# Tanh in place in bf16, the feed-forward's residual parked in DRAM, an eighth P slot with PV begun one round later, and retuned scheduler constants

## The chip, the cores and the metric

One core of a Trainium2 chip runs the whole kernel. The metric is the device time in microseconds (us) of one execution. PE is TensorE's matmul, PEld its weight load, DVE VectorE, ACT ScalarE, POOL GpSimd and SP SyncE, which issues the DMAs. Lines such as L708 are lines of the kernel's source; one helper records many operations, so the tile names beside a line say which operation it is. All the changed kernel's lines are one to seven higher than those of the kernel before: the exponential is L708 before and L709 after.

A median says how fast a kernel is, and a profile says where one execution spent its time.

## The reference

A transformer layer on 2048 tokens of 1024 features, 32 heads of 32, feed-forward width 3584, in bf16:

```python
qkv = (x @ wqkv).reshape(B, S, 3, H, Dh) ...          # on layernorm(x)
scores = jnp.einsum("bhqd,bhkd->bhqk", q, k) * scale
p = _softmax(scores, axis=-1)
o = jnp.einsum("bhqk,bhkd->bhqd", p, v)
h = x + o.reshape(B, S, D) @ wo
g = _gelu(jnp.einsum("bsd,df->bsf", _layernorm(h), w1) + b1)   # tanh form
h2 = h + jnp.einsum("bsf,fd->bsd", g, w2) + b2
```

## The kernel before

The program records every operation as a task with an assumed cost, lets a scheduler put the tasks of each engine in an order, and only then emits them. On the chip every engine runs its list in order. The scheduler's constants are therefore part of the kernel: they never appear in it as instructions, but they decide the order.

Attention is cut into 64 jobs (8 head groups by 8 chunks of 256 queries), each of 8 rounds. A round is one QK task (8 row-tiled matmuls), two exponentials of 128x1024 on ACT, and one PV task with its denominator (8 and 4 column-tiled matmuls). The exponentials write into a ring of P slots, from which PV reads:

```python
NPT = 7
PT, B_PT_ = sb(top, "PT", [P, NPT, 4, 512], BF, 2 * NPT)
...
EXP = (0.922, 0.907)                     # assumed cost of the two exps of a round
...
pe(fns, 0.217, reads=[B_KT[g][r], B_QT[self.slot]], ..., kind="qk", mode="row")
for q in range(2):
    t = act(lambda a, u=u, q=q: a.activation(PT[:, s, 2*q:2*q+2, :], psum[:, 2*u:2*u+2, :], ACT.Exp, ...), 1024, ...)
    t.occ = EXP[q]
```

The feed-forward of a chunk runs as background on PE between the QKs of the next chunks ("ffn1" is the matmul with w1, "ffn2" the one with w2). Its gelu takes one tanh on ACT for each block of 1024 columns:

```python
def gelu(R, c, fc, nf):
    (sq, b_sq), (th, b_th) = R.sq.next(), R.th.next()
    ... # sq = xh*xh ; sq = (sq + C2)*xh      (DVE)
    act(lambda a: a.activation(th, sq, ACT.Tanh, ...), n, reads=[b_sq], writes=[b_th], ...)
    dve(lambda v: v.scalar_tensor_tensor(xh, v4(th), 1.0, xh, ALU.add, ALU.mult), ...)
```

The scheduler for PE takes a ready QK first, then PV (a job's first PV only when PV_START rounds wait), then background:

```python
PV_START = 5
AHEAD = 0.3
HOLD = 3
...
if qk is not None:
    return qk
if pv is not None and not (state["mode"] == "full" and bg is not None and full_array(bg[1]) and waiting < HOLD):
    ...
    if free and pv is pvs[n] and (waiting >= PV_START or last or bg is None):
        ...
        return pv
if bg is not None:
    ...
    return t
return warm
...
gr.schedule(pick_pe)
```

At the start, 56 dummy matmuls keep PE busy while the first inputs arrive. Whatever background is left after the last QK runs alone at the end: the tail.

The softmax here doesn't subtract the row's maximum and nothing guards it: scores larger than these inputs give would overflow.

## Time and profile before

| | kernel before |
|---|---|
| median of 4 runs | 1102.28 us (1101.57 to 1104.14) |
| profiled span | 1102.0 us |
| first exponential | 15.52 us |
| ACT waits more than 1.5 us for the last time at | 64.61 us |
| from there to the end of the last exponential | 960.56 us, of which ACT is busy 957.19 |
| last exponential | ends at 1025.17 us |
| last exponential to end | 76.83 us |

The table reads as three stretches that add up to the span: 64.61 + 960.56 + 76.83 = 1102.0. Each has its own limit. In the lead the limit is how soon the first scores exist, in the long middle it is ACT, in the tail PE. A microsecond saved on an engine that isn't the limit of its stretch saves nothing. The prediction below shows the lines that this rests on.

### The profile page before, as it was taken

The page shows a single profiled execution, that of the slowest core. Times are in us where ns is not written, and L with a number is a line of the kernel's source. Part 1 is how long each engine was busy: PE and PEld are TensorE (multiplying, and loading weights), DVE is VectorE, ACT ScalarE, POOL GpSimd, SP SyncE. Part 2 cuts the span into 40 slices and gives each one's busy share as a digit, 9 for nine tenths or more (in the row PEclk, how much of TensorE's full clock was granted, in tenths as well). Part 3 has the DMA queues.
Part 4 walks back from the last instruction along what each step waited for, and adds up shares of the span by engine and source line. Part 5 has one row for each costly group of instructions (what it writes and reads, how often), then busy time and mean ns, then how long its engine had stood idle before and what let it go on. Part 6 is the DMA issues. An engine that isn't in the chain of part 4 may idle for free.

```text
span 1102.0 us, 41713 instructions
## 1 busy us (share of the span) xinstructions
PE 1059.0 (96%) x19045; PEld 588.9 (53%) x19045; DVE 823.8 (75%) x1449; ACT 1022.6 (93%) x1135; POOL 20.2 (2%) x33
## 2 busy tenths in 40 slices
PE   6999999999999989999999999999999999999999
PEld 5645565554444645454554455455545554554485
DVE  6456666666867898888788887968887888787463
ACT  5889999999999999999999999999999999999251
POOL 1100000000000000000000000000000000000000
PEclk9999999999999989999999999999999999999999
DMA  6960100012332754466837684775677487968770
GB/s 193 194 181 2 41 3 3 3 40 86 105 103 79 221 145 142 153 204 179 245 103 238 134 253 116 239 211 147 202 181 226 119 253 197 286 174 259 211 248 20
DMA packets 263161, 169.15 MB, mean 153 GB/s; under 512 B 50762, under 2 KB 260810, under 8 KB 262986
## 3 DMA queue, kind: packets, MB, share of 16 engines
q1 hardware_dynamic: 262986, 166.50, 52.8%
q8 instruction: 149, 2.44, 0.9%
q14 instruction: 26, 0.21, 0.1%
HBM read 152.31 MB, written 7.34 MB: 145 GB/s over the span
## 4 chain that ended last, share of the span: by engine, by line
ACT 78%; PE 18%; DVE 2%; DMA 1%; issue 0%; POOL 0%; DVEq 0%
ACT PT L708 74%; PE ps L504 9%; PE ps L501 5%; ACT a_th L846 4%; PE ps L700 2%; PE ps L720 2%; PE ps L739 1%; DMA w2r<-in_B_w_dram 1%; DMA hnT<-xb 1%; ACT xnT L583 0%; DMA xrb<-in_A_x_dram 0%; DVE xb L573 0%; DVE hch L785 0%; DVE stg L593 0%; DVE PS L715 0%
## 5 line engine op out<-in xcount | busy, mean ns | idle before, releaser
L708 ACT ACTIVATE PT<-ps 128x1024 bf16<-128x1024 f32 x1024 | 952.8, 1108 | 14.7 <-PE ps L700 14.2
L715 DVE TENSOR_TENSOR PS<-PT 128x1024 bf16<-128x1024 bf16 x495 | 333.1, 685 | 100.7 <-ACT PT L708 70.5
L700 PE MATMUL ps<-QT,KT 32*128 32x256 bf16 x4096 | 204.3, 274 | 14.1 <-ACT PT L708 13.1
L504 PE MATMUL ps<-hnT,w1r 128*128 128x256 bf16 x1632 | 210.8, 275 | 4.2 <-DVE gT L828 3.2
L501 PE MATMUL ps<-w2r,gT 128*32 128x512 bf16 x2832 | 192.0, 383 | 2.6 <-DVE a_os L871 1.6
L720 PE MATMUL ps<-PT,V 128*32 128x256 bf16 x4096 | 184.1, 275 | 6.6 <-ACT PT L708 5.0
L504 PEld LDWEIGHTS ps<-hnT,w1r 128*128 128x128 bf16 x1632 | 146.5, 98 | 59.3 <-issue 34.4
L700 PEld LDWEIGHTS ps<-QT,KT 32*128 32x128 bf16 x4096 | 61.3, 92 | 165.2 <-ACT PT L708 135.9
L739 PE MATMUL ps<-PS,ones 128*32 128x256 bf16 x1980 | 139.5, 276 | 1.6 <-DVE PS L715 1.6
L501 PE MATMUL ps<-xnT,Wall 128*32 128x512 bf16 x1888 | 126.7, 381 | 3.3 <-DVE stg L593 1.6
L720 PEld LDWEIGHTS ps<-PT,V 128*32 128x32 bf16 x4096 | 93.0, 96 | 66.2 <-ACT PT L708 28.9
L501 PEld LDWEIGHTS ps<-w2r,gT 128*32 128x32 bf16 x2832 | 66.1, 96 | 66.2 <-issue 26.7
L828 DVE TENSOR_TENSOR gT<-ps,b1f 128x512 bf16<-128x512 f32 x98 | 67.2, 685 | 23.0 <-PE ps L504 22.4
L504 PE MATMUL ps<-Wall,xnT 128*128 128x128 bf16 (+1 forms) x896 | 68.8, 228 | 1.2 <-ACT xnT L583 0.7
L739 PEld LDWEIGHTS ps<-PS,ones 128*32 128x32 bf16 x1980 | 52.3, 96 | 31.2 <-DVE PS L715 14.5
L501 PEld LDWEIGHTS ps<-xnT,Wall 128*32 128x32 bf16 x1888 | 43.1, 96 | 48.3 <-issue 16.0
L847 DVE SCALAR_TENSOR_TENSOR gT<-a_th,gT 128x1024 bf16<-128x1024 f32 x49 | 59.7, 1218 | 4.6 <-ACT a_th L846 4.3
L504 PEld LDWEIGHTS ps<-Wall,xnT 128*128 128x128 bf16 x896 | 55.0, 98 | 14.9 <-issue 9.5
L501 PE MATMUL ps<-w1r,OT 128*32 128x512 bf16 x896 | 60.9, 381 | 1.6 <-DVE hch L785 1.6
L844 DVE SCALAR_TENSOR_TENSOR a_sq<-a_sq,gT 128x1024 bf16<-128x1024 bf16 x49 | 59.8, 1220 | 0.6
L846 ACT ACTIVATE a_th<-a_sq 128x1024 f32<-128x1024 bf16 x49 | 56.9, 1160 | 0.0
L748 DVE STREAM_TRANSPOSE DT<-ps 128x256 f32<-128x256 f32 x64 | 28.5, 446 | 20.2 <-PE ps L739 19.8
(76 smaller groups left out, 573.4 us busy)
## 6 DMA issues: line engine op xcount, KB each, us to landing
w2r<-in_B_w_dram SPq DMA_DIRECT2D x105, 512.0 KB, 6.0
w1r<-in_B_w_dram SPq DMA_DIRECT2D x102, 512.0 KB, 4.3
w1r<-in_A_wo_dram SPq DMA_DIRECT2D x28, 512.0 KB, 4.3
wk<-in_B_w_dram SPq DMA_DIRECT2D x9, 512.0 KB, 6.2
xrb<-in_A_x_dram SPq DMA_DIRECT2D x16, 256.0 KB, 4.5
Wall<-in_A_wqkv_dram SPq DMA_DIRECT2D x16, 256.0 KB, 5.5
wv<-in_B_w_dram SPq DMA_DIRECT2D x8, 512.0 KB, 6.3
a_x<-in_A_x_dram SPq DMA_DIRECT2D x28, 128.0 KB, 4.3
```

The source lines that it names most:

```text
L501: fns.append(lambda p, j=j: p.matmul(dst(32 * j, 32 * j + 32), lhsT[:, 32 * j:32 * j + 32], rhs, start=start, stop=stop, tile_position=(0, ...
L504: t.alt = [lambda p: p.matmul(dst(0, P), lhsT, rhs, start=start, stop=stop, skip_group_check=True)]
L700: fns.append(lambda p, i=i, hh=hh, r0=r0: p.matmul(psum[:, 2 * us[hh // 2] + hh % 2, 256 * i:256 * i + 256], KT[r0:r0 + 32, g, 256 * r + P ...
L708: t = act(lambda a, u=u, q=q: a.activation(PT[:, s, 2 * q:2 * q + 2, :], psum[:, 2 * u:2 * u + 2, :], ACT.Exp, bias=0.0, scale=SCALE), 102 ...
L715: dve(lambda v: v.tensor_tensor(PS[:, z, :, :], PT[:, s, :, 0:256], PT[:, s, :, 256:512], ALU.add), c_dve(1024, 2), reads=B_PT[s], writes= ...
L720: fns.append(lambda p, i=i, hh=hh: p.matmul(psum[32 * hh:32 * hh + 32, self.bank, 0:256], V[:, g, 2 * r + i, 32 * hh:32 * hh + 32], PT[:, ...
L739: fns.append(lambda p, i=i, hh=hh, src=src: p.matmul(psum[32 * hh:32 * hh + 32, self.bank, 256:512], ones32[:, :], src[:, hh, :], start=False,
L748: dve(lambda v: v.transpose(DT[f][:], psum[:, self.bank, 256:512]), c_dve_ps(256), reads=[self.buf], writes=[B_DT[f]], prio=-1)
L828: gate[c] = dve(lambda v, xh=xh, fc=fc, grp=grp: v.tensor_tensor(xh, psum[:, grp.bank, :].rearrange("p (f n) -> p f n", f=2), b1f[:, fc:fc ...
L844: dve(lambda v: v.scalar_tensor_tensor(v4(sq), v4(sq), C2, xh, ALU.add, ALU.mult), c_dve(n), reads=[b_sq] + b_xh, writes=[b_sq], prio=1)
L846: gate[c] = act(lambda a: a.activation(th, sq, ACT.Tanh, bias=0.0, scale=K2 / 2), n, reads=[b_sq], writes=[b_th], prio=-1, kind="tanh")
L847: t = dve(lambda v: v.scalar_tensor_tensor(xh, v4(th), 1.0, xh, ALU.add, ALU.mult), c_dve(n), reads=[b_th] + b_xh, writes=b_xh, prio=1)
```

## The change

The intent is to free SBUF (tanh writes over its own input in bf16; the residual goes to DRAM and back) for an eighth P slot. With eight slots a job's PV may begin when six rounds wait, not five, so that PE can do its background in longer runs. At the same time the scheduler's constants were retuned and the warm-up was made longer.

```diff
-    NPT = 7
+    NPT = 8
...
-    hch, B_hch_ = sb(ffn, "hch", [P, 2, 2, D], BF, 8)
-    B_hch = [B_hch_[:4], B_hch_[4:]]
+    hch, B_hch = sb(ffn, "hch", [P, 2, D], BF, 4)
...
-    R1.sq = Ring(ring(ffn, "a_sq", 1, 1024, BF))
-    R1.th = Ring(ring(ffn, "a_th", 1, 1024, F32))
+    R1.sq = Ring(ring(ffn, "a_sq", 2, 1024, BF))
...
+    hd = nc.dram_tensor("h_scratch", [NC - 1, 2, P, D], BF, kind="Internal").ap()
...
-    EXP = (0.922, 0.907)
+    EXP = (0.9163, 0.9013)
...  (ln2_tile)
+        if c < NC - 1:
+            dma(hd[c, t], h, P * D * 2, reads=B_hch[2 * t:2 * t + 2], writes=[B_hd[c][t]], prio=1)
...  (gelu)
-        gate[c] = act(lambda a: a.activation(th, sq, ACT.Tanh, bias=0.0, scale=K2 / 2), n, reads=[b_sq], writes=[b_th], prio=-1, kind="tanh")
+        gate[c] = act(lambda a: a.activation(sq, sq, ACT.Tanh, bias=0.0, scale=K2 / 2), n, writes=[b_sq], prio=-1, kind="tanh")
...  (ffn2)
+            if not tail:
+                dma(o[:], hd[c, t, :, at], P * 1024, reads=[B_hd[c][t]], writes=[bo], prio=1)
+                h_ap, b_h = o[:], bo
...
-    for k in range(56):
+    for k in range(110):
-        pe(lambda p: ..., 0.1, ..., kind="warm")      # assumed cost
+        pe(lambda p: ..., 0.07, ..., kind="warm")
...
-    PLAN = [F2[0], 2, F2[1], 5, F2[2], 5, F2[3], 2]
+    PLAN = [F2[0], 3, F2[1], 4, F2[2], 5, F2[3], 2]
...
-    PV_START = 5
-    AHEAD = 0.3
+    PV_START = 6
+    AHEAD = 0.15
...
-    gr.schedule(pick_pe)
+    gr.schedule(pick_pe, switch=0.11382196630878494)
```

`switch` is the assumed cost of a change of PE's tiling mode; left out, it is 0.108.

More of the change, by code (lines that the diff above doesn't have):

```diff
@@ L434, in build_kernel @@
     w1r, B_w1r = sb(ffn, "w1r", [P, NW1, 2048], BF, NW1)
-    hch, B_hch_ = sb(ffn, "hch", [P, 2, 2, D], BF, 8)
-    B_hch = [B_hch_[:4], B_hch_[4:]]
+    hch, B_hch = sb(ffn, "hch", [P, 2, D], BF, 4)
     x_lo = ffn.cur
     R1.x = Ring([(h, [b]) for h, b in ring(ffn, "a_x", 2, 512, BF)])
-    R1.xb = Ring(ring(Area(x_lo), "xb2", 1, D, BF))
+    R1.xb = Ring(ring(ffn, "xb2", 1, D, BF))
     LN2_PRIO = -2
@@ L458, in build_kernel @@
     B_qd = [[gr.buf() for _ in range(3)] for _ in range(G)]
+    hd = nc.dram_tensor("h_scratch", [NC - 1, 2, P, D], BF, kind="Internal").ap()
+    B_hd = [[gr.buf() for _ in range(2)] for _ in range(NC - 1)]
     MM = 0.2150
@@ L784, in wo_group @@
             mm(grp, OT[:, c % NOT, g, t * P:t * P + P], w[:, g % 4, :], g == 0, g == G - 1, [B_OT[c % NOT][g], bw])
-        dve(lambda v: v.tensor_tensor(hch[:, c % 2, t, 512 * j:512 * j + 512], psum[:, grp.bank, :], x3, ALU.add),
-            c_dve_ps(512), reads=[grp.buf] + bx, writes=[B_hch[c % 2][2 * t + j]], prio=-2)
+        dve(lambda v: v.tensor_tensor(hch[:, t, 512 * j:512 * j + 512], psum[:, grp.bank, :], x3, ALU.add),
+            c_dve_ps(512), reads=[grp.buf] + bx, writes=[B_hch[2 * t + j]], prio=-2)
     def wo(R, c):
@@ L795, in ln2_tile @@
         o, bo = R.xb.next()
-        layer_norm([(hch[:, c % 2, t, :], B_hch[c % 2][2 * t:2 * t + 2], o, bo)], LN2_PRIO)
+        layer_norm([(hch[:, t, :], B_hch[2 * t:2 * t + 2], o, bo)], LN2_PRIO)
         if evac == "dma":
@@ L800, in ln2_tile @@
             transposes(group(f"t{c}.{t}"), o, bo, hnT[:, t, :, :], B_hnT[t], evac)
-        h = hch[:, c % 2, t, :]
+        h = hch[:, t, :]
         dve(lambda v: v.tensor_tensor(h, h, b2b[:], ALU.add), c_dve(1024, 2),
-            reads=[B_b2b], writes=B_hch[c % 2][2 * t:2 * t + 2], prio=2)
+            reads=[B_b2b], writes=B_hch[2 * t:2 * t + 2], prio=2)
+        if c < NC - 1:
+            dma(hd[c, t], h, P * D * 2, reads=B_hch[2 * t:2 * t + 2], writes=[B_hd[c][t]], prio=1)
     def ln2(R, c, evac):
@@ L807, in ln2 @@
             ln2_tile(R, c, t, evac)
+    GP = 1
     soft, gate = {}, {}
@@ L835, in gelu @@
     def gelu(R, c, fc, nf):
-        (sq, b_sq), (th, b_th) = R.sq.next(), R.th.next()
+        sq, b_sq = R.sq.next()
         n = 256 * nf
@@ L842, in v4 @@
             return ap.rearrange("p (f n) -> p f n", f=nf)
-        dve(lambda v: v.tensor_tensor(v4(sq), xh, xh, ALU.mult), c_dve(n, 2), reads=b_xh, writes=[b_sq], prio=1)
+        dve(lambda v: v.tensor_tensor(v4(sq), xh, xh, ALU.mult), c_dve(n, 2), reads=b_xh, writes=[b_sq], prio=GP)
         dve(lambda v: v.scalar_tensor_tensor(v4(sq), v4(sq), C2, xh, ALU.add, ALU.mult), c_dve(n),
-            reads=[b_sq] + b_xh, writes=[b_sq], prio=1)
-        gate[c] = act(lambda a: a.activation(th, sq, ACT.Tanh, bias=0.0, scale=K2 / 2), n, reads=[b_sq], writes=[b_th], prio=-1, kind="tanh")
-        t = dve(lambda v: v.scalar_tensor_tensor(xh, v4(th), 1.0, xh, ALU.add, ALU.mult), c_dve(n),
-                reads=[b_th] + b_xh, writes=b_xh, prio=1)
+            reads=[b_sq] + b_xh, writes=[b_sq], prio=GP)
+        gate[c] = act(lambda a: a.activation(sq, sq, ACT.Tanh, bias=0.0, scale=K2 / 2), n, writes=[b_sq], prio=-1, kind="tanh")
+        t = dve(lambda v: v.scalar_tensor_tensor(xh, v4(sq), 1.0, xh, ALU.add, ALU.mult), c_dve(n),
+                reads=[b_sq] + b_xh, writes=b_xh, prio=GP)
         soft.setdefault(c, set()).add(t)
@@ L869, in ffn2 @@
             o, bo = R.os.next()
-            h_ap, b_h = hch[:, c % 2, t, at], B_hch[c % 2][2 * t + j]
+            h_ap, b_h = hch[:, t, at], B_hch[2 * t + j]
+            if not tail:
+                dma(o[:], hd[c, t, :, at], P * 1024, reads=[B_hd[c][t]], writes=[bo], prio=1)
+                h_ap, b_h = o[:], bo
             dve(lambda v, o=o, h_ap=h_ap, grp=grp: v.scalar_tensor_tensor(
@@ L898, in build_kernel @@
         x_tile(tt, -6)
-    for k in range(56):
-        pe(lambda p: p.matmul(psum[:, 6, 0:P], ident[:], ident[:], start=True, stop=True), 0.1,
+    for k in range(110):
+        pe(lambda p: p.matmul(psum[:, 6, 0:P], ident[:], ident[:], start=True, stop=True), 0.07,
            reads=[B_ident], writes=[B_ps[6]], kind="warm")
@@ L1007, in build_kernel @@
     R2.sq = Ring(ring(tail, "b_sq", 3, 1024, BF))
-    R2.th = Ring(ring(tail, "b_th", 3, 1024, F32))
     R2.os = Ring(ring(tail, "b_os", 3, 512, BF))
```

## The prediction

> **What bounds the kernel now.** I read the busy summary first, then the busy time by stretches of 25 us, then the waits of ACT, then the chain that ended last in order of time, then single stretches. The busy summary:
>
> ```profile
> span 1102.0 us, 41713 instructions
> PE 1059.0 (96%) x19045; PEld 588.9 (53%) x19045; DVE 823.8 (75%) x1449; ACT 1022.6 (93%) x1135; POOL 20.2 (2%) x33
> ```
>
> Two engines are nearly full, so the share alone doesn't say which one counts. The stretches do; the columns are span of the stretch, PE, PEld, DVE, ACT, POOL busy, granted clock, DMA share, GB/s:
>
> ```profile
> 50.00:75.00 25.00, 24.50 (x468) 12.40 (x470) 10.23 (x21) 20.55 (x25) 0.00 (x0) 1.00 0.89 225
> 75.00:100.00 25.00, 24.22 (x500) 14.56 (x500) 17.33 (x32) 25.00 (x28) 0.00 (x0) 1.00 0.06 21
> 400.00:425.00 25.00, 21.36 (x333) 10.62 (x331) 20.57 (x31) 23.68 (x27) 0.00 (x0) 0.80 0.48 120
> 1000.00:1025.00 25.00, 22.51 (x430) 11.32 (x431) 16.43 (x25) 23.43 (x26) 0.00 (x0) 0.93 0.61 186
> 1025.00:1050.00 25.00, 24.93 (x162) 12.37 (x151) 10.94 (x25) 3.05 (x5) 1.54 (x2) 1.00 0.89 272
> ```
>
> There are three phases. Up to 64.6 us is a lead with gaps on ACT. From 64.6 to 1025.2 us ACT is the bound, full in all but a few stretches. From 1025 on ACT has almost nothing and PE runs what is left of the feed-forward: the tail, 77 us. The waits of ACT between 66 and 1026 us come to 3.1 us in 3 waits, against 960 us of work. The chain and two lines of ACT's timeline give the prices (start, length, what):
>
> ```profile
> 10.68 4.46 PE ps L504 x24
> 15.52 1.94 ACT PT L708 x2
> 64.61 249.88 ACT PT L708 x272
> 1015.85 9.32 ACT L708 ACTIVATE PT<-ps 128x1024 bf16<-128x1024 f32 x10 [1.43 <-PE ps L700]
> 1042.71 56.77 PE ps L504 x396
> ```
>
> One exp costs 249.88/272 = 0.919 us of ACT, a round (two exps) 1.84 us. The last exp ends at 1015.85 + 9.32 = 1025.2. In the tail PE waits for nothing the profile can see.
>
> **What the skill says.** (1) "TensorE: Matmul & The Clock Gate", Part 1: the array runs at half clock until it has been busy for a window of about 3.4 us, and falls back after an idle one. The trace agrees, and it costs time in three places. In the lead the 16 + 8 projection matmuls at 10.68 take 4.46 us, though 24 of 256 columns at full rate (0.109 us each, from 14 in 1.53 us elsewhere in the chain) take 2.6; granted clock there:
>
> ```profile
> 9.00:12.00 3.00, 1.88 (x17) 1.40 (x18) 3.00 (x7) 1.02 (x1) 0.00 (x0) 0.85 1.02 363
> 12.00:15.00 3.00, 3.00 (x17) 2.04 (x15) 1.26 (x5) 0.38 (x1) 0.49 (x1) 0.58 0.50 186
> ```
>
> The other two are at 407 to 417 us and 1011 to 1014 us, both at 0.50. Each follows rounds in which PE has only QK and PV and no background, and each is followed by one of the ACT waits, about 1.3 and 1.43 us. (2) "TensorEngine Tiling (Array Packing)", Key Properties: changing the tiling mode drains the array. The trace agrees: 8 PV matmuls take 0.22 us in the chain behind their own kind and 0.33 behind another, so a change costs 0.11 us. (3) "ScalarE: Activation LUTs", What ACT_TABLE_LOAD costs: one element per cycle for every function, fp32 and bf16 alike. Tanh and exp here agree, 0.94 and 0.92 us in the chain, so a bf16 result should not shorten the tanh. [...]128 KB to DRAM landed in a median of 1.7 us (queries parked) and 4.5 us (results)[...].
>
> **The change part by part.**
>
> Tanh in place, bf16: 56 calls, same count, same input, same length: 0. The multiply that reads it takes 1218 ns with an fp32 operand; the one before it, all bf16, takes 1220:
>
> ```profile
> L847 DVE SCALAR_TENSOR_TENSOR gT<-a_th,gT 128x1024 bf16<-128x1024 f32 x49 | 59.7, 1218 | 4.6 <-ACT a_th L846 4.3
> L844 DVE SCALAR_TENSOR_TENSOR a_sq<-a_sq,gT 128x1024 bf16<-128x1024 bf16 x49 | 59.8, 1220 | 0.6
> ```
>
> So DVE gains nothing. What is gained is room: 2 KB a partition here, and 4 KB from halving the residual tile, less 2 KB for an LN tile with its own place, which is the 4 KB of the eighth P slot. Two slots also let a second gelu block start before the first ends.
>
> Residual in DRAM: 14 stores of 256 KB and 28 loads of 128 KB, 7.3 MB on 169 MB. The instruction order has 70 more rows on SP. DMA share stays mostly below 0.9 in the ACT phase; all of it is beside other work: 0, unless SP's in-order queue holds a weight load (a rival).
>
> Warm-up: 110 instead of 56 dummy matmuls. From the instruction order, 79 stand before the first transposes, 26 between them and the second, 5 after. In the trace 24 ran in the first 2.5 us (0.103 us each, half clock), the other 31 in about 1.9 us (0.06). So 79 end near 1.52 + 2.5 + 55 x 0.06 = 7.3 us, against a first transpose at 6.9 now (+0.4); the other 26 end near 9.3, against 8.9 now (+0.3). In return the gap without PE work, most of 6.1 to 10.7 us now, shrinks to about 1 us, the clock should stay up, and the 24 matmuls take 2.6 instead of 4.46: -1.9. Sum: about -1.6 us at the first exp. Does it reach 64.6? DVE's layer-norm chain waits 1.74 and 1.72 us for PE's first two Q projections, so it moves along; PE waits for no DMA in 12 to 66 us. The order of the lead is otherwise nearly that of before. I take **-1.5 us**.
>
> PV start, eighth slot, plan and the scheduler's own constants: they only reorder PE. ACT's list is the same (1024 exps and 42 tanh before the end of attention), and changes of mode are 1214 against 1215, so no switch is saved. What counts is what is left after the last QK. Counting rows of the instruction order, before: 8 column-packed steps (4 matmuls each) + 76 full-array matmuls of the second feed-forward matmul for the last-but-one chunk, 84 steps, and 2 PV rounds; after: 5 + 64 = 69 steps, and 5 PV rounds. A step is 0.2165 us (28 matmuls of 4 columns tiles, 7 steps, in 1.51 us), a PV round with its denominator 0.33. So 15 x 0.2165 - 3 x 0.33 = 3.25 - 0.99: **-2.2 us** in the tail. The rest of the tail is the same work. It is worth its full size only if ACT stays full, since those 2.2 us are squeezed into PE's gaps.
>
> ACT's waits: 3.1 us now, 2.7 of them behind clock dips. Rounds without background in the instruction order: before 200 to 203 and 505 to 506; after 198 to 201, 349 to 350 and 502 to 504. So the dips stay about where they are. I take **-0.3 us**, for a scheduler whose assumed exp (0.909 us mean, was 0.9145) is now further below the measured 0.919, which puts QK a little earlier.
>
> New waits in the tail: the 64 full-array steps now run without the fillers that stood between them, so the last two of the seven 512 KB weight blocks (6.0 us to landing, median) may come late: **+0.3 us**.
>
> Sum: -1.5 - 2.2 - 0.3 + 0.3 = -3.7 us on 1101.6, so about **1097.9 us**; I say 1097.5.
>
> **The rivals.**
> (a) *Denser PE starves ACT.* For it: PE is 96% busy; in the new order the longest work between two QKs is 3.7 us by my count, against 2.9 before. Against: that round holds two tanh (2 x 0.94 more for ACT), and PE waits 10.1 us for ACT before QK in the ACT phase. A starved ACT adds 3 to 6 us: 1101 to 1104.
> (b) *The DRAM round trip turns into a wait.* The load of the residual waits for one of two output slots, so for an earlier store; SP issues in order, and weight loads stand behind it. For it: SP's own list already shows 54 us behind the output multiply. Against: weights are fetched several us ahead. It would make the tail 1 to 4 us longer: about 1099 to 1102.
> (c) *The clock dips go.* With a later PV start and two gelu slots the rounds without background may be filled in practice, so that 2.7 us of ACT's waits disappear: about 1095. Or a new dip appears at round 349: +1.3.
> (d) *The lead's gain is lost* because DMA (share 0.99 from 25 to 50 us) sets the pace there: 1099.
>
> **Range and chances.** The ACT phase can't shrink by more than its 3.1 us of waits, the lead by about 2, the tail by about 3: the best case is near 1093. The worst likely case is (a) or (b) with the gains kept: near 1102. Range 1092.5 to 1101.5. Faster by over 2% means below 1079.6, which only a change of ACT's work could give: 0.02. Slower by over 2% needs 22 us of new waits: 0.01. Within 2%: 0.97.
>
> **What would show it.** Right: the first exp near 13.9 us, with the clock near 1.0 from 9 to 15 us; the last exp near 1023.4 with the same counts; last exp to end near 74.6 us; tanh at 0.94 us and its multiply at 1.22 us. Wrong: ACT waiting for QK well above 3.1 us between 66 us and the last exp (a); PE waiting for weights, or for the output multiply, in the tail (b); no waits behind low clock at all (c); a first exp that is early while the last is not (d).

## More of the kernel before

One more row of before is wanted later, that of the exponentials inside the middle stretch, by shape. Its columns are the count, busy us, the mean ns of one record, the idle time ahead of them and who ended it:

```profile
L708 ACT ACTIVATE PT<-ps 128x1024 bf16<-128x1024 f32 x992 | 921.7, 1110 | 6.2 <-PE ps L700 6.0
```

## The result, and the profile after

The kernel after takes 1098.68 us (median of 4 runs, 1096.95 to 1099.43) against 1102.28 us before. The ratio is 0.9963, with an interval of 0.9944 to 0.9981. Ratios here are the mean time of one kernel's runs over that of the other's runs of the same rounds, so they differ a little from the ratio of the medians. Executions over 1.5% slower than the fastest of the same kernel are left out of the means. The interval lies below 1. The profiled execution of after took 1098.32 us, near its median; its span of 1096.5 us leaves out 1.8 us at the ends. That of before took 1103.84 us, 1.6 us over its median. So the 5.5 us between the two profiles overstate the 3.6 us between the medians.

The busy summary of after; the engines do the same work in a span that is 5.5 us shorter:

```profile
span 1096.5 us, 41949 instructions
PE 1062.1 (97%) x19130; PEld 589.0 (54%) x19135; DVE 822.9 (75%) x1449; ACT 1021.6 (93%) x1135; POOL 17.8 (2%) x33
```

The busy time by stretches of after (span, PE, PEld, DVE, ACT, POOL busy, granted clock, DMA share, GB/s):

```profile
9.00:12.00 3.00, 2.07 (x31) 1.84 (x29) 2.97 (x8) 1.15 (x2) 0.00 (x0) 1.00 1.06 374
12.00:15.00 3.00, 3.00 (x34) 2.31 (x32) 2.22 (x9) 1.27 (x2) 0.70 (x1) 1.00 0.45 163
...
400.00:425.00 25.00, 22.29 (x356) 13.33 (x360) 23.12 (x36) 25.00 (x28) 0.00 (x0) 0.93 0.53 143
1000.00:1025.00 25.00, 23.22 (x459) 10.79 (x448) 14.40 (x25) 21.10 (x23) 0.00 (x0) 0.93 0.69 215
1025.00:1050.00 25.00, 24.89 (x150) 14.04 (x152) 10.49 (x23) 3.73 (x6) 1.54 (x2) 1.00 0.95 292
```

The clock now stays at 1.00 from 9 to 15 us. It still falls near 405 and near 1005 us; the first fall costs ACT nothing this time (25.00 of 25.00 busy), the second costs 1.40 us. The chain of after in order of time (start, length, what), with its last line from the timeline of ACT:

```profile
1.53 6.09 PE ps L907 x79
11.17 2.56 PE ps L505 x22
14.11 1.94 ACT PT L709 x2
63.26 302.67 ACT PT L709 x330
...
1009.56 12.94 ACT L709 ACTIVATE PT<-ps 128x1024 bf16<-128x1024 f32 x14 [1.40 <-PE ps L701]
```

The last exponential ends at 1009.56 + 12.94 = 1022.50. So the three stretches are 63.26, 959.24 and 74.00 us: 1.35, 1.32 and 2.83 us shorter than before, 5.5 in all. PE's waits in the last of them come to one line, so no weight is late:

```profile
PE ps L505 <- issue: 0.2, 1, 0.2
```

The tanh and the multiply that reads it, from the page of after. The multiply's second operand is now bf16, and it still takes 1222 ns:

```profile
L851 DVE SCALAR_TENSOR_TENSOR gT<-a_sq,gT 128x1024 bf16<-128x1024 bf16 x49 | 59.9, 1222 | 12.3 <-ACT a_sq L850 11.8
L850 ACT ACTIVATE a_sq<-a_sq 128x1024 bf16<-128x1024 bf16 x49 | 58.9, 1203 | 0.0
```

The surprise is in the row of the exponentials in the middle stretch, which answers to the one shown of before:

```profile
L709 ACT ACTIVATE PT<-ps 128x1024 bf16<-128x1024 f32 x992 | 922.7, 1168 | 5.8 <-PE ps L701 5.7
```

The mean record of an exponential got longer, 1168 against 1110 ns. Yet ACT's busy time over that stretch, for the same 1041 instructions (992 exponentials and 49 tanh), fell from 957.19 to 956.23 us. The Trainium skill, "ScalarE: Activation LUTs", What ACT_TABLE_LOAD costs, says that back-to-back ACTIVATEs overlap by about 93 ns. This trace agrees: two exponentials that had to wait for their scores take 1.94 us, and 330 that never did take 302.67, or 0.917 each; the first one of a pair costs 1.94 - 0.917 = 1.02, so 0.10 more. An exponential whose scores are ready early starts inside the record of the one before it, so its own record is longer. How much of that helps is in the records between 66 us and the last exponential. Where a record overlaps the one before by 0.10 us or more, it ends 0.917 us after it in the mean, in both kernels and however long the overlap. Where it overlaps by less, or waits, its step is longer. There are 41 such records of about 1040 in the kernel before and 21 in the kernel after; beyond the waits themselves they cost ACT 1.95 us and 1.04 us. After's QKs come with more **slack**. The mean of the records tells that they start earlier; it isn't a cost, and read as one it would have told the opposite.

### The profile page after: what moved, and what is told of

Read it like the earlier page. It is cut to its first block, busy times and chain, and to the rows that moved or that the text cites. A ratio compares the mean times of both kernels' runs of the same rounds, so it can differ in the third digit from the quotient of the medians.

```text
span 1096.5 us, 41949 instructions
## 1 busy us (share of the span) xinstructions
PE 1062.1 (97%) x19130; PEld 589.0 (54%) x19135; DVE 822.9 (75%) x1449; ACT 1021.6 (93%) x1135; POOL 17.8 (2%) x33
## 3 DMA queue, kind: packets, MB, share of 16 engines
q8 instruction: 150, 2.46, 0.9%
## 4 chain that ended last, share of the span: by engine, by line
ACT 83%; PE 15%; DMA 1%; DVE 1%; issue 0%; POOL 0%; POOLq 0%; DVEq 0%
ACT PT L709 79%; PE ps L505 8%; ACT a_sq L850 4%; PE ps L502 3%; PE ps L701 1%; PE ps L721 1%; DMA hnT<-xb 1%; PE ps L907 1%; PE ps L740 1%; DVE PS L716 0%; ACT xnT L584 0%; PE ps L581 0%; DVE gT L851 0%; ACT V L592 0%; DVE a_os L878 0%
## 5 line engine op out<-in xcount | busy, mean ns | idle before, releaser
L716 DVE TENSOR_TENSOR PS<-PT 128x1024 bf16<-128x1024 bf16 x495 | 327.6, 686 | 83.1 <-ACT PT L709 49.5
L721 PE MATMUL ps<-PT,V 128*32 128x256 bf16 x4096 | 180.9, 275 | 5.9 <-ACT PT L709 5.0
L851 DVE SCALAR_TENSOR_TENSOR gT<-a_sq,gT 128x1024 bf16<-128x1024 bf16 x49 | 59.9, 1222 | 12.3 <-ACT a_sq L850 11.8
L850 ACT ACTIVATE a_sq<-a_sq 128x1024 bf16<-128x1024 bf16 x49 | 58.9, 1203 | 0.0
```

Of the source, the lines that this page charges most:

```text
L716: dve(lambda v: v.tensor_tensor(PS[:, z, :, :], PT[:, s, :, 0:256], PT[:, s, :, 256:512], ALU.add), c_dve(1024, 2), reads=B_PT[s], writes= ...
L721: fns.append(lambda p, i=i, hh=hh: p.matmul(psum[32 * hh:32 * hh + 32, self.bank, 0:256], V[:, g, 2 * r + i, 32 * hh:32 * hh + 32], PT[:, ...
L850: gate[c] = act(lambda a: a.activation(sq, sq, ACT.Tanh, bias=0.0, scale=K2 / 2), n, writes=[b_sq], prio=-1, kind="tanh")
L851: t = dve(lambda v: v.scalar_tensor_tensor(xh, v4(sq), 1.0, xh, ALU.add, ALU.mult), c_dve(n), reads=[b_sq] + b_xh, writes=b_xh, prio=GP)
```

## The experiments

Each ran on one chip with the kernel before beside it, and the ratio is to that. The four runs of the first group shared 11 runs of before (median 1103.14 us), the next four 11 (1102.82), the next three 11 (1104.21), the last one 11 (1104.02).

Four numbers are read from each profile: the start of the middle stretch, its length and busy time on ACT, and the time from the last exponential to the end. The middle begins after the last long wait of the lead; single waits of 1.6 to 1.7 us later on (two in e1, one in e4) count in the middle.

| profiled execution | lead | middle | ACT busy in it | tail | span | ratio of its runs |
|---|---|---|---|---|---|---|
| before | 64.61 | 960.56 | 957.19 | 76.83 | 1102.0 | 1 |
| after | 63.26 | 959.24 | 956.23 | 74.00 | 1096.5 | 0.9963 |
| e1 after, old warm-up | 64.47 | 961.00 | 955.89 | 73.93 | 1099.4 | 0.9963 |
| e2 before, new warm-up | 63.74 | 959.47 | 957.13 | 76.69 | 1099.9 | 1.0008 |
| e3 after, old constants | 65.92 | 962.04 | 957.37 | 76.64 | 1104.6 | 1.0034 |
| e4 before, new constants | 62.64 | 956.13 | 951.58 (5 tanh fewer) | 109.23 | 1128.0 | 1.0222 |
| e5 after again | 65.47 | 955.76 | 955.56 | 73.87 | 1095.1 | 0.9952 |
| e6 warm-up in the gaps | 64.31 | 959.23 | 955.97 | 73.96 | 1097.5 | 0.9959 |
| e7 no residual in DRAM | 62.95 | 955.53 | 955.50 | 73.92 | 1092.4 | 0.9951 |
| e8 no clock falls | 63.48 | 958.65 | 956.42 | 74.77 | 1096.9 | 0.9959 |

### e1: the kernel after with the warm-up of before

```diff
     gr.assign(sems, lanes)
+    warms = [t for t in gr.seqs[E.PE] if t.kind == "warm"]
+    for k, t in enumerate(warms):
+        if not (k < 55 or k == 79) and not t.inc:
+            t.fns = []
```

> The kernel after, with the warm-up of before: 55 dummy matmuls before the first transposes and one between them in place of 79 and 26; the order of all other instructions is the kernel after's. Theory 1 (lead and tail add up, each on its own): the first exponential goes back from 14.1 to about 15.5 us, the start of the stretch in which ScalarE never waits long from 63.3 to about 64.6, the time from the last exponential to the end stays at 74.0, so about 1.3 us longer than the kernel after: about 1100.0. Rival (what the lead gains is lost again further on, in waits for the weights and the inputs): the kernel after's own time, 1098.7.

Measured: 1099.46 us (6 runs, 1096.23 to 1101.55), ratio 0.9963 [0.9945, 0.9981]. The first exponential did go back, and the 22 projection matmuls again ran at a low clock (the chain of this run):

```profile
10.72 4.23 PE ps L505 x22
15.33 1.94 ACT PT L709 x2
```

The tail stayed at 73.93. So the tail's gain doesn't need the new warm-up. Whether the lead's gain is lost can't be told from the medians: this one lies 0.8 us above that of after's first runs and 2.1 us above that of e5 below, and the intervals overlap.

### e2: the kernel before with the warm-up of after

```diff
     gr.assign(sems, lanes)
+    warms = [t for t in gr.seqs[E.PE] if t.kind == "warm"]
+    warms[54].fns = warms[54].fns * 25
+    warms[55].fns = warms[55].fns * 26
```

> The kernel before, with the warm-up of after: 79 dummy matmuls before the first transposes and 26 between them; the order of all other instructions is the kernel before's. Theory 1: the first exponential comes forward from 15.5 to about 14.1 us, the tail stays at 76.8, so about 1.3 us shorter than before: about 1101.0. Rival (the lead's gain is lost again): 1102.3, no difference.

Measured: 1103.79 us (6 runs, 1101.50 to 1108.14), ratio 1.0008 [0.9986, 1.0029]. The profiled execution has its first exponential at 14.56 and is 2.1 us shorter than the profile of before, but the other runs give that back. The rival fits the median; a gain of 1.3 us would lie at the edge of the interval. A likely reason comes with e5.

### e3: the kernel after with the scheduling constants of before

```diff
-    EXP = (0.9163, 0.9013)
+    EXP = (0.922, 0.907)
-    PLAN = [F2[0], 3, F2[1], 4, F2[2], 5, F2[3], 2]
+    PLAN = [F2[0], 2, F2[1], 5, F2[2], 5, F2[3], 2]
-    AHEAD = 0.15
+    AHEAD = 0.3
-    gr.schedule(pick_pe, switch=0.11382196630878494)
+    gr.schedule(pick_pe)
```

> The kernel after with the four scheduling constants of before (exponential cost 0.922 and 0.907, look-ahead 0.3, the old switch penalty, plan 2,5,5,2), so only its structure: bf16 tanh in place, feed-forward residual in DRAM, eighth P slot with PV two rounds later, new warm-up. Its instruction order leaves after the last QK 2 PV rounds and 84 column steps, as the kernel before. Theory 1: the lead gain of 1.3 us is kept and the tail's is gone: last exponential to end about 76.8, about 1101.0 in all. Rival (the structure itself makes the gain, the constants are mere labels): 1098.7.

Measured: 1106.72 us (6 runs, 1104.44 to 1110.46), ratio 1.0034 [1.0014, 1.0053]. The structure alone, with bf16 tanh, residual in DRAM, eighth slot and later PV, is no gain; it is a little slower than before. The tail is 76.64 us, as the count of work left (84 steps, as before) said, and ACT's busy time in the middle is 957.37, as before, with 46 records that overlap by less than 0.10 us: the slack went with the constants. That the run is slower than before and not merely equal was not expected. In the profiled execution 2.6 us of it can be named: the lead is 1.3 us later and ACT waits 1.3 us more in the middle. The lead, from the chain of this run:

```profile
1.52 6.97 PE ps L907 x79
...
20.23 3.17 PE ps L505 x14
```

The 79 dummy matmuls took 6.97 us, not 6.09, and 14 projection matmuls at 20.23 us 3.17 us, which take 1.70 in the profile of after: the clock had fallen again. The waits of the middle hold two pauses of PE that nothing in the profile caused, 0.90 us at 725 and 1.34 us here (the timeline of PE):

```profile
930.80 0.38 PE L502 MATMUL ps<-w2r,gT 128*32 128x512 bf16 x2
932.52 0.61 PE L502 MATMUL ps<-w2r,gT 128*32 128x512 bf16 x6 [1.34 <-issue]
```

More on these pauses below. Whether both causes hold in all six runs isn't known.

### e4: the kernel before with the scheduling constants of after

The edit is e3's diff the other way round, made to the kernel before.

> The kernel before with the four scheduling constants of after and nothing else, so the old warm-up, seven P slots, f32 tanh, residual in SBUF. Its instruction order leaves after the last QK 3 PV rounds, 140 column steps of the feed-forward and seven blocks of the step before it: 43.8 us by the durations of the trace, against 18.8 for the kernel before. Theory 1 (the tail follows the count of work left): last exponential to end about 100 us, the last exponential some 3 us earlier, 1121 to 1125 in all. Rival (the constants only relabel and ScalarE's total decides): 1099 to 1103.

Measured: 1127.76 us (4 runs), ratio 1.0222 [1.0204, 1.0241]. The count was right in kind: 25.0 us more by the count, 32.4 us more in the profile. The 7.4 us on top come from a tail that now had its own trouble: PE waits 3.1 us in it for the layer norm of the last chunk and 1.1 us for weights, and the clock was at half for 6.8 us, which costs about half of that. This stretch shows it low:

```profile
1047.00:1051.00 4.00, 2.89 (x13) 1.74 (x15) 3.85 (x6) 1.29 (x3) 0.05 (x1) 0.51 1.05 283
```

In the middle, this run has only 17 records that overlap by less than 0.10 us. So the new constants bring the slack to the old structure too, and pay for it in the tail.

Neither the structure nor the constants gain anything alone. With seven slots and PV at five rounds, the new constants make the scheduler push work into the tail; with eight slots and PV at six, they don't. One rival was not run: the new constants and PV at six with seven slots. Building the kernel after with `NPT = 7` gives an order that leaves the same 69 steps and 5 PV rounds after the last QK. So the eighth slot, for which the tanh and the residual were changed, isn't shown to be needed.

### e5: the kernel after again, on the chip of e6 to e8

> The kernel after unchanged, to have it on the same chip in the same rounds as the three kernels beside it. Both theories: 1098.7, a ratio to before near 0.9963. Its lead is open: in the five executions profiled so far whose clock rose at different moments, the 79 dummy matmuls took 6.1 to 7.0 us, so the first exponential may be anywhere from 14.1 to 15.1 us.

Measured: 1097.37 us (6 runs, 1095.16 to 1100.55), ratio 0.9952 [0.9934, 0.9969]. The profiled execution is the best lesson on the lead. The timeline of PE at its start:

```profile
1.53 7.32 PE L907 MATMUL ps<-ident 128*128 128x128 bf16 x79 [1.53 <-POOL ident L532]
```

The same 79 dummy matmuls took 7.32 us here and 6.09 us in the first profile of the same kernel. By the clock records of the two traces, the clock rose to full at 7.3 us here and at 4.7 us there. Over the fourteen profiled executions it rose anywhere from 4.2 to 7.5 us. So the first exponential came at 15.34 us, and the middle began at 65.47, later than in the profile of before. With the lead's gain turned into a loss of 0.9 us, this execution is still 6.9 us shorter than that of before: 4.8 us from the middle, where ACT waited 0.2 us in all, and 3.0 us from the tail.

The old warm-up has the same lottery with other prizes, by the three executions that have it. When the clock rises early, its 55 dummies end early, PE idles and the clock falls before the projections (before and e1). When it rises late, they end just in time, nothing falls, and the first exponential comes at 13.53 us (e4). The new warm-up never lets the clock fall there, but makes the first transposes late: at 7.22 to 8.79 us, against 6.8 to 6.9. But the clock can still fall later in the lead, as here at 27.8 us. That is what sorts the leads of all fourteen profiles: in the five in which it doesn't fall there at all (after, e2, e4, e7, e8) the middle begins at 62.6 to 63.7 us, in the nine in which it does, at 64.3 us or later. Three of the four profiles of after's instruction order with its warm-up (after, e5, e7, e8) are among the five.

### e6: the dummy matmuls in the gaps

```diff
+    warms = [t for t in gr.seqs[E.PE] if t.kind == "warm"]
+    for k, t in enumerate(warms):
+        if 55 <= k < 79 and not t.inc:
+            t.fns = []
+        if k > 104:
+            t.fns = t.fns * 3
```

> The kernel after with its warm-up dealt out otherwise: 55 dummy matmuls before the first transposes (as before), 26 between the two sets of transposes, 15 after them in the gap up to the first projections. Theory 1 (the new warm-up keeps the clock up but makes the transposes late, and the lead goes straight into the total): first transposes at 6.9 us in place of 7.6, the 22 projection matmuls at full clock in 2.6 us from about 10.7, first exponential near 13.5, about 0.6 to 1.5 us shorter than the kernel after: about 1097.5. Rival (the lead's place in the total is lost to the executions' own scatter, or to DMA): no difference from the kernel after.

Measured: 1098.93 us (6 runs, 1096.38 to 1100.12), ratio 0.9959 [0.9943, 0.9976]. The timeline of PE shows the lead that was wanted:

```profile
1.52 5.12 PE L907 MATMUL ps<-ident 128*128 128x128 bf16 x55 [1.52 <-POOL ident L532]
6.92 0.62 PE L581 MATMUL ps<-ident,xb 128*128 128x128 bf16 x8 [0.28 <-DVE mvr L553]
...
10.80 1.91 PE L505 MATMUL ps<-xnT,Wall 128*128 128x256 bf16 x16 [0.37 <-ACT xnT L584]
```

The first exponential came at 13.75, as theory 1 had it. But the middle stretch began at 64.31 us: the clock fell at 19.1 us in this execution, further on in the lead. The total doesn't differ from after's. The first exponential is a poor mark for the lead.

### e7: no store and load of the residual

```diff
-        if c < NC - 1:
-            dma(hd[c, t], h, P * D * 2, ...)
-                dma(o[:], hd[c, t, :, at], P * 1024, ...)
-                h_ap, b_h = o[:], bo
+                h_ap, b_h = b2b[:, at], B_b2b
```

> The kernel after without the store and the load of the feed-forward's residual (wrong result on purpose: the second bias is added in its place). Theory 1 (the DRAM round trip lies beside other work): 0 within 1 us of the kernel after, tail 74.0, instruction order on TensorE and ScalarE the same. Rival (it costs waits for the output slot, or slows the weights): 1 to 4 us shorter, 1095 to 1098, with fewer pauses of ScalarE.

Measured: 1097.90 us (6 runs, 1094.24 to 1100.27), ratio 0.9951 [0.9932, 0.9970], beside e5's 0.9952 on the same chip; the result is wrong, as intended. The 7.3 MB of DRAM traffic cost nothing that these runs can see. The profiled execution, 1092.4 us, is one in which ACT never waited more than 0.15 us between 66 us and the last exponential; that one execution isn't proof of an effect, since the medians of e5 and e7 lie 0.5 us apart with the intervals on top of each other.

### e8: no falls of the clock

```diff
+            qk.fill = lambda p: p.matmul(psum[:, 2 * us[0], 0:256], ident[:], KT[:, g, 256 * r:256 * r + 256], start=True, stop=True)
...
+    for k, t in enumerate([t for t in gr.seqs[E.PE] if t.kind == "qk"]):
+        if k in (198, 199, 200, 201, 202, 502, 503, 504, 505):
+            t.fns = [t.fill] * 4 + t.fns
```

> The kernel after with four full-array filler matmuls of 256 columns in front of the QK of the nine rounds that have no feed-forward work (rounds 198 to 202 and 502 to 505), written to the QK's own bank and overwritten by it; all else in the same order. Theory 1 (the falls of the granted clock at 404 to 414 and at 1004 to 1011 us are made by these rounds, and ScalarE's waits behind them by the low clock): clock 1.00 through both stretches, ScalarE's waits of 1.3 to 1.7 us at 413 to 418 and of 1.4 at 1009 to 1016 gone, 1.4 to 3 us shorter than the kernel after: about 1096.5. Rival (the clock falls anyway, or the fillers make the QK late): the same as the kernel after or 0.5 to 1 us longer.

Measured: 1098.74 us (5 runs, 1097.49 to 1099.72), ratio 0.9959 [0.9944, 0.9975]. The fillers do what they should to the clock. The stretches of the two falls in this run (their clock is 0.57 and 0.60 in after), and the timeline of PE in one of its rounds:

```profile
404.00:408.00 4.00, 3.21 (x47) 1.81 (x48) 3.55 (x6) 3.79 (x5) 0.00 (x0) 1.00 0.41 84
1004.00:1008.00 4.00, 3.26 (x66) 1.73 (x64) 2.06 (x3) 4.00 (x5) 0.00 (x0) 1.00 0.74 227
```

```profile
1008.20 0.61 PE L707 MATMUL ps<-KT,ident 128*128 128x256 bf16 x4
1008.74 0.40 PE L701 MATMUL ps<-QT,KT 32*128 32x256 bf16 x8
```

The falls are gone. Those near 1005 us are missing in the profiles of e5 and e7 too, without fillers; but the one near 405 us is in every other profile of after's order, and the mean granted clock of all five runs is 0.998 to 1.000, against 0.994 to 0.998 in the six of e5. So the rounds without background made them.

The time isn't shorter. A filler stands between the release of the QK's bank and the QK: in the round shown it makes the QK 0.54 us later (1008.20 to 1008.74), and ACT waits 0.91 us behind it; between 400 and 412 us ACT is busy for 11.40 of 12.00 us, where it was busy all the time in e5. Two of the nine rounds, 202 and 505, do have background ahead of them, and the round shown is 505: 40 feed-forward matmuls lie between the QK before it and its filler, so this filler wasn't needed. The tail also has a pause of 0.57 us of the kind that e3 showed. In this profile at least, the fillers spend slack. The rival was right about the time.

### e9: the order with the least work in the tail

```diff
-    EXP = (0.9163, 0.9013)
+    EXP = (0.92425, 0.90925)
-    PV_START = 6
+    PV_START = 7
-    HOLD = 3
+    HOLD = 4
-    gr.schedule(pick_pe, switch=0.11382196630878494)
+    gr.schedule(pick_pe, switch=0.10806901002562994)
```

> The kernel after with other scheduling constants (assumed exponential 0.924 and 0.909, switch penalty 0.108, PV three rounds later than before, HOLD 4): an order that leaves 55 steps and 2 PV rounds after the last QK, against 69 and 5. Both theories: the time from the last exponential to the end 74.0 - 14 x 0.2165 - 3 x 0.33 = about 70.0 us. Theory 1 (the tail's count of work decides, ScalarE's phase stays as it is): about 1094. Theory 2 (a slack theory: so much background is squeezed between the QKs that they come only just in time, ScalarE's exponentials lose their overlap with the one before, and every pause of TensorE goes through to ScalarE): its ScalarE busy time for the same 1041 instructions goes from 955.5 to 956.4 up to 957 or more, the recorded mean of an exponential falls from about 1175 to 1110 ns or less, ScalarE's waits grow by 2 to 5 us, and the total is 1097 to 1101.

Measured: 1104.80 us (6 runs, 1103.69 to 1107.24), ratio 1.0010 [0.9993, 1.0026], so 5 to 6 us longer than after by the ratios, and beyond even theory 2. ACT's row in the middle stretch:

```profile
L709 ACT ACTIVATE PT<-ps 128x1024 bf16<-128x1024 f32 x992 | 921.9, 1097 | 7.5 <-PE ps L701 7.3
```

The mean record fell to 1097 ns, ACT's busy time for the 1041 instructions of the middle rose to 958.90 us, 70 records overlap by less than 0.10 us (before 41, after 21), and the waits over 0.15 us after 66 us come to 5.5. That is the slack theory. A second cause plays in: the clock fell three times in the middle of this profile, and 1.9 us of the waits stand behind a low clock (the six runs have a mean granted clock of 0.983 to 0.988). The extra cost of the records with too little overlap, 3.68 us against 1.04 in after, is not of that kind: 2.72 us of it lie in records that neither wait nor stand near a low clock, against 0.61 in after. The tail also kept its 74.24 us instead of 70.0, which neither theory had. Its reason is a pause just after the last exponential (timeline of PE):

```profile
1027.76 0.82 PE L502 MATMUL ps<-w2r,gT 128*32 128x512 bf16 x11
1030.65 1.87 PE L502 MATMUL ps<-w2r,gT 128*32 128x512 bf16 x17 [2.07 <-issue]
```

After a pause of 2.07 us the clock was low for 3.4 us, which by this estimate costs about half of that: 70.0 + 2.07 + 1.7 = 73.8.

### e10: constants chosen for slack and tail together

```diff
-    EXP = (0.9163, 0.9013)
+    EXP = (0.92623, 0.91123)
-    PLAN = [F2[0], 3, F2[1], 4, F2[2], 5, F2[3], 2]
+    PLAN = [F2[0], 3, F2[1], 5, F2[2], 4, F2[3], 2]
-    AHEAD = 0.15
+    AHEAD = 0.5
-    gr.schedule(pick_pe, switch=0.11382196630878494)
+    gr.schedule(pick_pe, switch=0.12742)
```

> The kernel after with constants chosen for both (assumed exponential 0.926 and 0.911, look-ahead 0.5, switch penalty 0.127, plan 3,5,4,2; PV start as in after): 60 steps and 4 PV rounds after the last QK, 22 fewer changes of tiling mode (1192 against 1214), so 22 x 0.11 = 2.4 us less TensorE time in ScalarE's phase. Both theories: last exponential to the end 74.0 - 9 x 0.2165 - 0.33 = about 71.7 us. Theory 1 (only the tail): about 1096. Theory 2 (slack): ScalarE busy 955.5 to 956 as in after, mean of an exponential at or above 1170 ns, total 1094.5 to 1096.5, and shorter than the run with 55 steps beside it although its tail is longer.

Measured: 1098.87 us (6 runs, 1097.14 to 1102.36), ratio 0.9953 [0.9934, 0.9973]. It is 5.9 us shorter than e9 beside it, although its order leaves more work for the tail; that part of theory 2 holds, and the mean record in the middle is 1172 ns. It isn't better than after, and the total misses the expected range. The tail took 75.92 us in the profile, not 71.7, by the same kind of pause at the same place:

```profile
1024.88 0.38 PE L740 MATMUL ps<-PT,ones 128*32 128x256 bf16 x5
1027.20 0.29 PE L740 MATMUL ps<-PT,ones 128*32 128x256 bf16 x3 [1.94 <-issue]
```

```profile
1028.00:1032.00 4.00, 4.00 (x13) 1.49 (x11) 2.21 (x5) 0.00 (x0) 0.00 (x0) 0.57 0.11 37
```

The pause cuts a task of eight matmuls in two, and the program puts waits on semaphores only ahead of a task's first instruction. The page of after has a line for a queue that carries instructions:

```profile
q8 instruction: 150, 2.46, 0.9%
```

PE's 19,130 matmuls and 19,135 weight loads, divided by 150 packets, give 255 to a packet. The Trainium skill, "Runtime: NRT & Kernel Launch", Instruction fetch mechanics, says that an engine's instructions come in blocks of 16 KiB, 256 instructions, fetched while the current block runs, and that the cost of crossing a boundary is mostly hidden. The block size agrees with the trace (2.46 MB / 150 = 16.4 KB). "Mostly hidden" doesn't hold for PE here. In the profiles there are 16 such pauses of more than 0.4 us, and PE went on 2.3 to 3.2 us after a packet of this queue was issued in every one of the 16, while the median distance of packets is 6.7 to 7.0 us. That pointed to a wait for the next block, and made a test possible.

The traces show still more. Number PE's matmuls, weight loads and sequencer instructions by their records, as if none were missing: each of the 16 pauses stands in front of number 192 or 193 of a run of 256, and there are as many such places as packets (149 in before, 150 in after). So all of them are at the boundary of a block. The scheduler of both kernels already has such boundaries in its model (`fetch=4.7`: a block may begin 4.7 us after the last one at the earliest), but it counts matmuls and weight loads alone. At the pause in the tail of e10, 184 sequencer instructions are missing from its count, so it places the boundaries elsewhere.

### e11: PV one round earlier, as before

```diff
-    PV_START = 6
+    PV_START = 5
```

> The kernel after with PV of a job beginning two rounds earlier, as in before (the eighth P slot is then never needed, all else as after). Its order leaves 140 steps, 2 PV rounds and three blocks of the first feed-forward matmul after the last QK. Theory 1: tail 74.0 + 71 x 0.2165 - 3 x 0.33 + 3 x 1.745 = 93.6, or some us more where the longer tail waits for weights (it was 7 us over the count in the run of before with new constants), last exponential 2 to 4 us earlier because tanh calls move behind it: 1114 to 1124. Rival (the PV start only reorders and the time stays): 1098.

Measured: 1119.48 us (4 runs, 1117.68 to 1119.99), ratio 1.0136 [1.0118, 1.0154]; tail 97.19 us, last exponential at 1020.41, 2.1 us earlier than after. The later PV start is what makes the new constants usable. It is worth 20 us to them, and by e3 nothing to the old ones. In this order at most six rounds are outstanding when a QK is issued.

### e12: e10 with fifty instructions fewer ahead

```diff
+    warms = [t for t in gr.seqs[E.PE] if t.kind == "warm"]
+    for k, t in enumerate(warms):
+        if (55 <= k < 79 or 99 <= k < 105) and not t.inc:
+            t.fns = []
+        if k > 104:
+            t.fns = t.fns * 2
```

> The kernel of the run with more slack, with the dummy matmuls dealt out as 55, 20 and 10 in place of 79, 26 and 5: 25 fewer, so 50 instructions fewer in TensorE's stream ahead of everything else; the order is otherwise the same. It tests the reading that TensorE's 1.94 us pause just after the last exponential in that run is a wait for its next 256 instructions (128 matmuls with their weight loads): they would end 50 instructions later, behind the dense run of PV and denominator matmuls. Theory: no pause and no low clock behind it, last exponential to the end about 71.9 us in place of 75.9, first exponential near 13.8 us in place of 15.6, total 1094.5 to 1096.5. Rival (the pause has another cause, at that place): tail near 75.9 again and 1098 to 1099.

Measured: 1097.69 us (6 runs, 1096.73 to 1098.61), ratio 0.9942 [0.9924, 0.9960]. The order around the last exponential is that of e10, and the pause isn't there (timeline of PE):

```profile
1024.53 0.39 PE L740 MATMUL ps<-PT,ones 128*32 128x256 bf16 x8
1025.09 0.81 PE L505 MATMUL ps<-wk,OT 128*128 128x512 bf16 x3 [0.17 <-issue]
```

The tail is 71.96 us, as expected (71.9), against 75.92, and the first exponential came at 13.79 us. Nothing was changed but the number and place of dummy matmuls a millisecond earlier, and the pause went. This is one execution of each, but both the place and the size were named beforehand. The total is 1 to 3 us above what was expected; in this profile the middle began only at 65.40 us and PE made three pauses of the same kind in it (0.97, 1.60 and 0.89 us). This version has the lowest ratio of all. It is faster than before, but its interval overlaps that of after (0.9934 to 0.9969, on another chip), so it isn't shown to beat it.

## Why the prediction was right, point by point

The total was right: 1097.5 predicted, 1098.68 measured, inside the range, and within 2%. The change was right as well, -3.7 us by the sum against -3.6 by the medians, and its largest term, the tail, came about by the mechanism that was named. That the sum fits so closely is partly luck: the term for ACT was about 1 us too small, the weight waits of 0.3 us didn't come, and the lead's 1.5 us come in some executions only. The terms fared as follows.

**Tail, -2.2 us.** Right, and a little small: 76.83 and 76.69 us in the two profiles of before's order, 73.87 to 74.00 in the five that have after's (after, e1, e5, e6, e7). That is -2.8 us, the most repeatable part of the change. The reading that PE waits for nothing in before's tail isn't quite right: the chain of before goes through a weight load there (6.73 us from 1035.93), and PEld waits 0.3 us for it. Counting what the order leaves after the last QK was a good method for these orders, and e4 and e11 bear it out in kind with 20 to 32 us at stake. e9 and e10 show its limit: the count doesn't see a pause of PE.

**New weight waits in the tail, +0.3 us.** They didn't come: the tail of after has no wait for a weight.

**ACT's waits, -0.3 us.** This is the term that was mis-sized. The mechanism was named ("puts QK a little earlier"), but only waits long enough to see were counted. The larger effect is in the exponentials that overlap the one before by less than 0.10 us: ACT's busy time for the same 1041 instructions is 957.1 to 957.2 us with before's order and 955.5 to 956.2 with after's, so -1.3 us by the means of 2 and 5 profiles. The waits came to 3.1 and 2.2 us with before's order and from 0.0 to 5.1 with after's, so they are mostly scatter: of the 2.9 us of after, 1.40 stand behind a low clock and 1.55 behind three pauses of PE. e9, whose order leaves less for the tail and no slack, shows that this term can decide more than the tail.

**Lead, -1.5 us.** Right for the profiled pair (-1.35), not shown as a property of the kernel. The prediction took the moment at which the clock rises from one trace as if it were fixed. The traces show that it isn't: the clock rose between 4.2 and 7.5 us, and after's own lead is 63.26 us in one execution and 65.47 in another. e1 (old warm-up on after) and e2 (new warm-up on before) find no effect on the total, but their intervals, some 0.2% or 2 us to either side, wouldn't show one of 1.3 us.

**Tanh in bf16: 0, DRAM round trip: 0.** Both right. The multiply takes 1222 ns against 1218, and e7 finds no difference without the round trip.

**The rivals.** (a), denser PE starving ACT, didn't happen in after, but is most of what sank e9. (b) fell with e7. (c): the clock's fall near 405 us stayed, the one near 1005 us is in three of the five profiles with after's order (after, e1, e6), and in e8 taking them away by fillers gained nothing. (d), the lead's gain lost, happened in some executions, with a fall of the clock each time; that DMA did it isn't shown.

**Which part of the diff gains.** The prediction left it with the order as a whole, and that stands: by e3, e4 and e11 the later PV start and the constants gain only together. Whether the room is needed for that was not tested (e4).

**What stays open.** It is not settled why e3 is slower than before by 0.34%, with all six runs above before's median; its one profile names 2.6 us of lead and waits. That the pauses are waits for the instruction stream rests on their timing and their place (16 of 16 each) and on one shift that removed one of them as foretold; what makes a block late in one execution and not in the next isn't known. Which of the four constants brings the slack wasn't tried either.

## What to carry to other kernels

When one engine sets the pace, look not only at its waits but at how early its inputs are ready: here the same 1041 instructions took 1.3 us less with more slack, with longer records, and an order that traded slack for less work at the end was 5.9 us slower than the one beside it. Constants of a scheduler belong to the structure they were tuned for, so test them together and apart before crediting either. And where something varies from one execution to the next, such as the moment at which the clock rises, one profile of each version can't say what a change of a microsecond is worth; count executions.

## What the Trainium skill lacked or had wrong

- "Runtime: NRT & Kernel Launch", Instruction fetch mechanics, calls the crossing of a block boundary mostly hidden. Here PE paused 0.5 to 2.1 us at 16 places in 14 profiled executions, always at a boundary of 256 instructions and until 2.3 to 3.2 us after a 16 KB packet of the instruction queue was issued; a shift of 50 instructions removed a pause of 1.94 us (e10, e12).
- "TensorE: Matmul & The Clock Gate", Part 1, puts the fall of the clock down to an idle window. In the 14 profiles, the 36 falls from full to half clock (those at the very end of an execution left out) followed 3.41 us in which PE was still busy for 0.31 to 0.60 of the time (0.49 of it before the fall at 407 us in the kernel before). Cut into the same steps of 3.41 us, no stretch at full clock with more than 0.60 was followed by a fall, and about fifteen with 0.49 to 0.60 weren't either.
- The same part says that the window runs free of the kernel and that the ramp varies from run to run, which the prediction left unused. The runs agree (clock up at 4.2 to 7.5 us) and add what it costs a kernel with a short lead: 79 dummy matmuls took 5.9 to 7.4 us, and the first exponential of one and the same kernel came at 14.1 or 15.3 us.
- "ScalarE: Activation LUTs", What ACT_TABLE_LOAD costs, gives the overlap of back-to-back ACTIVATEs (about 93 ns; 0.10 us here), but not that the records in a profile overlap by up to 0.4 us, of which all beyond 0.10 us leaves the step at 0.917 us. So the mean record of an exponential rose from 1110 to 1168 ns while the busy time fell by 1 us.
- "TensorEngine Tiling (Array Packing)", Key Properties, gives no figure for the drain at a change of tiling mode; it is 0.11 us here (8 PV matmuls 0.33 us behind another mode, 0.22 behind their own).
